# Both heads of a lone pair multiply whole float32 v into one PSUM tile, and ACT squares q and k: attention and two mixers on one core

## The chip, the core and the metric

The kernel runs on one core of a Trainium2 chip. It is one program; its time is the device time of one execution in microseconds (us). Before the change three runs took 1522.56, 1524.37 and 1529.31 us, so the median is 1524.37 us.

Engine names in the rows: PE is TensorE (matmul), PEld its weight load, DVE is VectorE, ACT is ScalarE, POOL is GpSimd, SP is SyncE, which issues nearly all DMAs here.

## The reference

Attention over q, k, v of shape (4 batches, 12 heads, 448 tokens, 64), with an RMS norm on q and k, then two mixer blocks:

```python
q_n, k_n = (rmsnorm(q, g_q), rmsnorm(k, g_k))
scores = scale * np.matmul(q_n, k_n.transpose(0, 1, 3, 2))
scores = scores - np.max(scores, axis=-1, keepdims=True)
attn = np.exp(scores)
attn = attn / (np.sum(attn, axis=-1, keepdims=True) + 1e-09)
x = np.matmul(attn, v)          # then heads are joined: (4, 448, 768)

h = x.transpose(0, 2, 1) @ U @ V                 # block a: rank 32 over tokens
u = x + h.transpose(0, 2, 1)
x = u + np.maximum(u @ w_ch1, 0.0) @ w_ch2       # 768 -> 3072 -> 768

h = np.maximum(x.transpose(0, 2, 1) @ w_tok1, 0.0) @ w_tok2   # block b
u = x + h.transpose(0, 2, 1)
x = u + np.maximum(u @ w_ch1b, 0.0) @ w_ch2b     # 768 -> 1536 -> 768
```

The weights arrive as 64-bit floats, read as pairs of 32-bit words.

## The kernel before

Heads are worked two by two: a pair is two neighbouring heads of one batch, its tiles hold both. There are 24 pairs. The first 12 (batches 0 and 1) run by themselves, one head after another; these are the lone pairs. The other 12 (batches 2 and 3) are interleaved by `run` with the channel mixer `ffn` of block a on batches 0 and 1. After that no attention is left. All steps are emitted in the order of the Python loops, and a scheduler then orders each engine's own queue; the order on each engine is fixed when the program is built, and an engine carries out its queue in that order.

A lone head goes through these steps:

- `fetch_heads` and `load_pair`: q, k and v of a pair are loaded by SP as 112 x (2 heads x 4 chunks x 64). POOL (DVE in turns 0, 2 and 3) squares q and k into `sq`, DVE sums the squares into `ms`, small operations make the inverse norm `rs`, and POOL multiplies q and k by it into `qn` and `kn`.
- `turn_pair`: PE transposes qn and kn into `tt`; ACT and DVE cut each into a rounded part and a rest (`both`), and SP copies them to `qs` and `ks`, so that one matmul of depth 128 takes both parts.
- `softmax`: for each of 4 chunks of 112 queries, two matmuls make the scores `sc`; DVE takes the negative maximum `nm` (L459), ACT the exponential `p` with its sum (L461), POOL scales `p` (L468).
- `weigh`: for each of 4 chunks of 112 keys, PE transposes the four `p` into `pt` (L487). Then p times v is summed in `pv`.

The product with v has two forms. The odd head of a lone pair, and both heads of a later pair, take the **split** form: ACT copies pt to `ph` as float32r (L498), DVE makes the rest `pl` (L502), v is split by ACT and POOL into `vs`, and two float32r matmuls, ph and pl, go to pv. The product lies in two halves of pv, so ACT copies one to `tmp` (L510) and DVE adds the other (L511). The even head of a lone pair takes the **whole** form: `ph` is a plain float32 copy of pt, made by ACT and DVE in turn (L498, L496), and one float32 matmul with `vr` follows. The profile records each such float32 matmul twice. DVE copies 64 rows of pv to the result (L507).

PSUM has 8 banks. In the lone stage 3 hold sc, 1 tt, and 4 are shared by pt and pv (`pools["v"] = pools["p"]`).

After the last lone pair comes what is called the seam below: `rank_mix` of batches 0 and 1 (the rank-32 mixer: lines L570 to L605, tiles `pt_x`, `xs`, `ps_h`, `ps_u`, `xT`, `u`), and the first two chunks of each channel weight of block a. Such a chunk is 768 KB in `w_raw`; `to_f32` converts it (ACT L130 and L135, DVE L131, L132 and L136, POOL L139), `split` cuts it into two float32r tiles (ACT L149, POOL L150), and these are stored as `h_a` for use again.

## Time and profile before

| | |
|---|---|
| median of three runs | 1524.37 us |
| lowest, highest | 1522.56, 1529.31 us |
| span of the profiled execution | 1530.0 us |
| PE busy | 1440.5 us (94%) |
| DVE busy | 1177.0 us (77%) |
| ACT busy | 745.0 us (49%) |
| POOL busy | 908.4 us (59%) |
| mean granted TensorE clock | 0.982 of full speed |

The span runs from the first to the last instruction of the profiled execution. For that execution no time of its own is given beside its span; the span is 5.6 us over the median of the three runs and 0.7 us over the highest. Busy shares are means over stages with different limits, so the table alone doesn't say what a stage waits for. Durations of matmuls overlap; what PE takes for one is read from the distance of starts.

### The profile page before, as it was taken

To read this page: it belongs to the slowest core of one execution; us is meant where nothing else is said; L and a number is where in the kernel's file an instruction comes from. 1 tells how busy PE (TensorE), PEld (TensorE's weight loads), DVE (VectorE), ACT (ScalarE), POOL (GpSimd) and SP (SyncE) were. 2 spreads that over 40 slices of the span, in tenths; PEclk is the share of its full clock that TensorE was granted. 3 is DMA by queue.
4 is the path that set the end of the run, shared out by engine and by line. 5 is a ranking of instruction groups with operands and counts; after the bars stand their busy time and mean duration, and the time that the engine had idled before them with its cause. 6 is when DMAs were issued, how large, how long until landed. Compare 5 with 4: busy or idle time off the path is not lost.

```text
span 1530.0 us, 22086 instructions
## 1 busy us (share of the span) xinstructions
PE 1440.5 (94%) x7396; PEld 1274.2 (83%) x7396; DVE 1177.0 (77%) x1805; ACT 745.0 (49%) x1508; POOL 908.4 (59%) x943
## 2 busy tenths in 40 slices
PE   4899988999899999999999999999999999999998
PEld 3666767888788889888888998898999998988997
DVE  7898888977787788676757776477888988577786
ACT  4687765765565665444535343335343431334431
POOL 5889947777666565455655454037787855206842
PEclk9999989999999999999999999999999999999999
DMA  6676656866666565765637664354545363423433
GB/s 174 156 168 158 151 169 208 273 201 199 223 207 202 165 207 189 248 228 189 213 125 239 227 232 143 115 194 130 181 125 185 125 192 122 130 92 109 137 117 108
DMA packets 144385, 266.06 MB, mean 174 GB/s; under 512 B 12832, under 2 KB 104448, under 8 KB 144160
## 3 DMA queue, kind: packets, MB, share of 16 engines
q1 hardware_dynamic: 143952, 264.65, 55.4%
q8 instruction: 59, 0.97, 0.3%
q14 instruction: 54, 0.44, 0.1%
q10 hardware_dynamic: 320, 0.00, 0.0%
HBM read 149.72 MB, written 79.10 MB: 150 GB/s over the span
## 4 chain that ended last, share of the span: by engine, by line
PE 50%; DVE 9%; DMA 4%; ACT 3%; POOL 3%; issue 2%; SPq 0%; DVEq 0%; POOLq 0%; ACTq 0%
PE ps_x L79 23%; PE ps_p L79 10%; PE ps_g L79 10%; PE ps_t L79 2%; PE ps_u L79 2%; DVE w_bits L136 1%; DVE w_bits L131 1%; DVE w_bits L132 1%; PE pv L79 1%; ACT w_bits L130 1%; POOL w L150 1%; DMA w_raw<-in_moe_w_ch_dram 1%; PE pt L487 1%; DMA c_a<-w_bits 1%; DMA qs<-both 1%
## 5 line engine op out<-in xcount | busy, mean ns | idle before, releaser
L79 PE MATMUL ps_x<-gs,w 128*128 128x448 f32 x1440 | 326.2, 373 | 7.6 <-DVE gs L656 2.9
L79 PE MATMUL ps_g<-u,w 128*128 128x448 f32 x1440 | 313.3, 371 | 6.5 <-DVE u L583 2.6
L79 PEld LDWEIGHTS ps_x<-gs,w 128*128 128x128 f32 x1440 | 268.6, 191 | 33.7 <-DVE gs L656 5.8
L79 PEld LDWEIGHTS ps_g<-u,w 128*128 128x128 f32 x1440 | 270.5, 190 | 30.3 <-DVE u L583 3.5
L79 PE MATMUL ps_x<-gs,w_b 128*128 128x448 f32 x1026 | 228.7, 368 | 6.5 <-DVE xT L851 2.0
L139 POOL TENSOR_TENSOR w_bits<-w_bits,w_round 128x768 uint32<-128x768 uint32 (+3 forms) x80 | 145.0, 1812 | 119.9 <-DVE w_bits L136 68.3
L79 PEld LDWEIGHTS ps_x<-gs,w_b 128*128 128x128 f32 x1026 | 192.7, 189 | 24.7 <-DVE xT L851 3.4
L150 POOL TENSOR_TENSOR w<-w_bits,w 128x768 fp32r<-128x768 f32 (+3 forms) x82 | 148.1, 1815 | 83.0 <-ACT w L149 78.6
L686 DVE TENSOR_TENSOR xT<-ps_x,xT 128x448 f32<-128x448 f32 x216 | 132.3, 618 | 44.5 <-PE ps_x L79 42.1
L150 POOL TENSOR_TENSOR w_b<-w_f,w_b 128x384 fp32r<-128x384 f32 x104 | 118.8, 1155 | 61.5 <-ACT w_b L149 61.1
L79 PE MATMUL sc<-ks,qs 128*112 128x448 f32 x384 | 124.6, 410 | 20.1 <-ACT p L461 16.9
L468 POOL TENSOR_SCALAR p<-p,sm 112x448 f32<-112x448 f32 x192 | 131.2, 696 | 19.4 <-DVE sm L465 16.1
L300 POOL TENSOR_TENSOR w_f<-w_f 128x384 f32<-128x384 f32 x26 | 36.4, 1401 | 178.7 <-DVE pu L779 73.5
L461 ACT ACTIVATE p<-sc,nm 112x448 f32<-112x448 f32 x192 | 121.4, 635 | 39.1 <-DVE nm L459 37.6
L459 DVE TENSOR_REDUCE nm<-sc 112x1 f32<-112x448 f32 x192 | 116.1, 614 | 11.8 <-PE sc L79 11.3
L487 PEld LDWEIGHTS pt<-ident,p 112*112 112x112 f32 x768 | 89.6, 135 | 34.3 <-issue 12.7
L487 PE MATMUL pt<-ident,p 112*112 112x112 f32 x768 | 110.6, 262 | 4.8 <-DVE pl L502 3.7
L498 ACT ACTIVATE ph<-pt 112x448 fp32r<-112x448 f32 (+1 forms) x168 | 88.2, 544 | 38.9 <-PE pt L487 38.0
L131 DVE TENSOR_SCALAR w_bits<-w_bits 128x768 f32<-128x768 f32 (+3 forms) x80 | 66.7, 834 | 50.0 <-ACT w_bits L130 50.0
L135 ACT ACTIVATE w_round<-w_raw 128x768 uint32<-128x768 uint32 (+3 forms) x80 | 69.8, 873 | 66.9 <-POOL w_bits L139 62.4
L502 DVE TENSOR_TENSOR pl<-pt,ph 112x448 fp32r<-112x448 f32 x144 | 86.9, 615 | 19.2 <-ACT ph L498 18.7
L130 ACT ACTIVATE w_bits<-w_raw 128x768 f32<-128x768 f32 (+3 forms) x80 | 70.0, 875 | 58.7 <-POOL w L150 31.4
(141 smaller groups left out, 2724.1 us busy)
## 6 DMA issues: line engine op xcount, KB each, us to landing
w_raw<-in_moe_w_ch_dram SPq DMA_DIRECT2D x72, 768.0 KB, 5.2
w_b<-h_a SPq DMA_DIRECT2D x65, 384.0 KB, 4.2
h_a<-w SPq DMA_DIRECT2D x56, 384.0 KB, 2.7
ks<-both SPq DMA_DIRECT2D x92, 224.0 KB, 3.7
c_a<-w_bits SPq DMA_DIRECT2D x40, 384.0 KB, 4.8
w_f<-c_a SPq DMA_DIRECT2D x40, 384.0 KB, 3.1
h_b<-w SPq DMA_DIRECT2D x32, 384.0 KB, 2.5
w_b<-h_b SPq DMA_DIRECT2D x29, 384.0 KB, 3.9
```

The costliest lines, as they stand in the source:

```text
L79: nc.tensor.matmul(o, lhsT=l, rhs=r, start=start, stop=stop)
L130: nc.scalar.activation(f(w), f(high), AF.Abs)
L131: nc.vector.tensor_scalar_max(f(w), f(w), TINY)
L139: nc.gpsimd.tensor_tensor(w, w, r, op=ALU.add)
L150: nc.gpsimd.tensor_sub(lo, w, f(hi))
L459: nc.vector.tensor_reduce(nm, sc, axis=AX.X, op=ALU.max, negate=True)
L461: nc.scalar.activation(p, sc, AF.Exp, bias=nm, accum_out=sm[:, c % 2:c % 2 + 1])
L468: nc.gpsimd.tensor_scalar(x, x, sm[:, i:i + 1], 1.0, op0=ALU.mult, op1=ALU.mult)
L487: nc.tensor.transpose(pt[:, c * CP:(c + 1) * CP], pr[c][:, kc * CP:(kc + 1) * CP], ident[:CP, :CP],)
L498: nc.scalar.activation(ph, pt, AF.Copy)
L502: nc.vector.tensor_sub(pl, pt, f(ph))
L686: nc.vector.tensor_add(xT[:, dc], px, xT[:, dc])
```

## The change

In the lone pairs both heads take the whole form. v is loaded into one of four standing tiles of shape 112 x 4 x 3 x 64 whose middle 64 columns are zero. The even head multiplies the first 128 columns (v, 0), the odd head the last 128 (0, v), and all eight matmuls of the pair add up in one `pv` of 128 rows, which DVE copies out once. v's load becomes two DMAs for each pair, with runs of 256 B in place of 1024 B. pv gets a PSUM bank of its own, and pt keeps three. ACT squares q and k in all lone pairs but those of turns 0, 2 and 3, with one buffer for q and another for k. The later pairs are as before.

```diff
-            t = pools["at"].tile([CP, 2, NC4, D], F32, tag="vr" if nm == "v" else "qkr", bufs=AT[nm + "r"],
-                        name=f"{nm}r")
-            nc.sync.dma_start(t, dict(q=q, k=k, v=v)[nm][b, h0:h0 + 2].rearrange(
-                "h (p c) d -> p h c d", c=NC4))
+            src = dict(q=q, k=k, v=v)[nm][b, h0:h0 + 2].rearrange("h (p c) d -> p h c d", c=NC4)
+            if nm == "v" and padded:
+                w = padded.pop(0)
+                padded.append(w)
+                for j in range(2):
+                    nc.sync.dma_start(w[:, :, 2 * j], src[:, j])
...
-            sq = pools["at"].tile([CP, 2 * NC4, D], F32, tag="sq", bufs=AT["sq"], name="sq")
+            sq = pools["pp" if padded and i else "at"].tile([CP, 2 * NC4, D], F32, tag="sq", bufs=AT["sq"], name="sq")
             tt = t.rearrange("p h c d -> p (h c) d")
-            mul(sq, tt, tt)
+            if padded and turn not in (0, 2, 3):
+                nc.scalar.activation(sq, tt, AF.Square)
+            else:
+                mul(sq, tt, tt)
...
     def split_v(vr, whole):
+        if whole:
+            return [vr[:, :, j:j + 2].rearrange("p c h d -> p c (h d)") for j in range(2)]
...
-        pv = psum("v", [P, S], "pv")
+        pv = joint.pop() if whole and j else psum("v", [P, S], "pv")
+        if whole and not j:
+            joint.append(pv)
...
-                mm(pv, vj[:, kc * D:kc * D + P], ph, kc == 0, kc == NC4 - 1)
+                mm(pv, vj[:, kc], ph, j == 0 and kc == 0, j == 1 and kc == NC4 - 1)
...
-            nc.vector.tensor_copy(dst[j * D:(j + 1) * D], pv[:D])
+            if j:
+                nc.vector.tensor_copy(dst, pv)
...
-        open_pools(inner, (("pp", 1, 0), ("s", 3, 1), ("t", 1, 1), ("p", 4, 1)))
-        pools["v"] = pools["p"]
+        open_pools(inner, (("pp", 1, 0), ("s", 3, 1), ("t", 1, 1), ("p", 3, 1), ("v", 1, 1)))
+        padded = []
+        for i in range(4):
+            padded.append(pools["pp"].tile([CP, NC4, 3, D], F32, tag=f"vp{i}", name="vr"))
+            nc.gpsimd.memset(padded[i][:, :, 1], 0.0)
```

The change also moves instructions on every engine, since the scheduler orders anew. Three places are shown. The lines of the changed kernel have other numbers: L487 becomes L498, L496 becomes L507, L507 becomes L519, L577 becomes L589, L581 becomes L593, L583 becomes L595.

On PE, in the middle of the lone stage, an odd head of before reads (pv_2012 is the odd head's, pv_2098 the next even head's; x4 and x2 are that many matmuls in a row):

```order
L79 MATMUL sc_2141<-ks_1964,qs_1963 112x448 x2
L79 MATMUL sc_2216<-ks_1970,qs_1969 112x448 x2
L79 MATMUL pv_2012<-pl_2061,vs_1545 128x448
L79 MATMUL pv_2012<-ph_2081,vs_1545 128x448
L487 MATMUL pt_2117<-ident_67,p_1881 112x112
L487 MATMUL pt_2117<-ident_67,p_1896 112x112
L487 MATMUL pt_2117<-ident_67,p_1916 112x112
L487 MATMUL pt_2117<-ident_67,p_1931 112x112
L79 MATMUL pv_2098<-ph_2104,vr_1552 128x448
L79 MATMUL pv_2012<-pl_2083,vs_1545 128x448
```

With the change, where one pair ends and the next begins (pv_1363 is the next pair's):

```order
L79 MATMUL sc_1371<-ks_1214,qs_1213 112x448 x2
L425 MATMUL tt_1622<-ident_67,qn_1476 128x112 x4
L498 MATMUL pt_1417<-ident_67,p_1132 112x112
L498 MATMUL pt_1417<-ident_67,p_1147 112x112
L498 MATMUL pt_1417<-ident_67,p_1167 112x112
L498 MATMUL pt_1417<-ident_67,p_1182 112x112
L498 MATMUL pt_1488<-ident_67,p_1290 112x112
L498 MATMUL pt_1488<-ident_67,p_1304 112x112
L79 MATMUL sc_1391<-ks_1214,qs_1213 112x448 x2
L79 MATMUL pv_1363<-ph_1369,vr_118 128x448
L79 MATMUL pv_1363<-ph_1388,vr_118 128x448
L79 MATMUL pv_1363<-ph_1404,vr_118 128x448
```

The matmuls with pl are gone, all products read vr, and the products of two pairs no longer interleave, since there is one bank for pv.

On SP, the first weight chunk of block a stands before the change behind every load and copy of the lone pairs (qs_2833 and ks_2834 belong to the second later pair):

```order
L442 DMA qs_2833<-both_2822 64x448 x2
L364 DMA vr_2713<-in_v_dram 112x2x256
L441 DMA ks_2834<-both_2830 64x896 x2
L364 DMA kr_3540<-in_k_dram 112x2x256
L364 DMA qr_3987<-in_q_dram 112x2x256
L364 DMA vr_2852<-in_v_dram 112x2x256
L121 DMA w_raw_2874<-in_moe_w_ch1_dram 128x6x128
L364 DMA vr_3542<-in_v_dram 112x2x256
L364 DMA vr_3991<-in_v_dram 112x2x256
L175 DMA h_a1_0_2888<-w_2884 128x768
```

With the change the second and third chunk (2674, 2953) are issued here, among the copies of the ninth lone pair (qs_1638 and qs_1644), and the first, w_raw_2657, stands 16 rows ahead of them:

```order
L367 DMA vr_118<-in_v_dram 112x4x64
L175 DMA h_a1_0_2671<-w_2667 128x768
L449 DMA qs_1638<-both_1627 64x448 x2
L367 DMA vr_118<-in_v_dram 112x4x64
L175 DMA h_a1_0_2671<-w_2668 128x768
L121 DMA w_raw_2674<-in_moe_w_ch1_dram 128x6x128
L121 DMA w_raw_2953<-in_moe_w_ch2_dram 128x768
L371 DMA qr_2135<-in_q_dram 112x2x256
L449 DMA qs_1644<-both_1627 64x448 x2
```

So the weight loads have moved ahead by several pairs, past copies that the lone pairs wait for; the fourth follows 7 rows below.

On DVE, at the start of the seam, the row before the change (L511 ends the last lone pair; L577 begins rank_mix):

```order
L511 TENSOR_TENSOR xT_82<-pv_2769,tmp_2814 64x448
L577 TENSOR_TENSOR xs_2940<-pt_x_2936,xs_2940 112x384
L577 TENSOR_TENSOR xs_2949<-pt_x_2945,xs_2949 112x384
L131 TENSOR_SCALAR w_bits_2876<-w_bits_2876 128x768
L132 TENSOR_SCALAR w_bits_2876<-w_bits_2876 128x768
L136 SCALAR_TENSOR_TENSOR w_bits_2876<-w_raw_2874,w_bits_2876 128x768
L577 TENSOR_TENSOR xs_2958<-pt_x_2954,xs_2958 112x384
L577 TENSOR_TENSOR xs_2967<-pt_x_2963,xs_2967 112x384
L605 TENSOR_TENSOR xs_2972<-ps_h_2935,xs_2972 64x384
```

With the change:

```order
L519 COPY xT_82<-pv_2534 128x448
L589 TENSOR_TENSOR xs_2724<-pt_x_2720,xs_2724 112x384
L589 TENSOR_TENSOR xs_2733<-pt_x_2729,xs_2733 112x384
L589 TENSOR_TENSOR xs_2742<-pt_x_2738,xs_2742 112x384
L589 TENSOR_TENSOR xs_2751<-pt_x_2747,xs_2751 112x384
L617 TENSOR_TENSOR xs_2756<-ps_h_2719,xs_2756 64x384
```

The conversion of the first weight chunk has left this place. So have those of the next three: all twelve DVE instructions of the four chunks now stand ahead of the last lone pair's copy, and so do their ACT operations L130 and L135, their POOL additions L139, and the split of the first two. The fifth chunk's three DVE instructions stand near the end of the last rank_mix.

## Rows read from the trace of the kernel before

**Rows 1.** Busy us of each engine by stretch: two lone, seam, mixed.

```profile
core 0: us, PE busy (x) PEld busy (x) DVE busy (x) ACT busy (x) POOL busy (x), PEclk, DMA share, GB/s
...
52.00:186.00 134.00, 122.68 (x704) 90.74 (x703) 116.23 (x241) 102.19 (x280) 120.26 (x225) 0.99 0.65 160
186.00:194.00 8.00, 6.30 (x34) 4.01 (x32) 5.35 (x9) 4.58 (x10) 6.05 (x11) 0.98 0.67 206
194.00:234.00 40.00, 33.42 (x152) 26.35 (x153) 34.82 (x58) 26.49 (x49) 17.47 (x12) 0.88 0.53 177
234.00:617.00 383.00, 363.54 (x1958) 323.18 (x1957) 307.39 (x522) 233.12 (x482) 255.17 (x283) 0.98 0.65 204
```

**Rows 2.** Groups of PE from 52 to 186 us: busy, mean ns, idle before.

```profile
L79 PE MATMUL sc<-ks,qs 128*112 128x448 f32 x146 | 47.5, 415 | 6.3 <-ACT p L461 4.7 <-DMA ks<-both 1.5
...
L79 PE MATMUL pv<-ph,vr 112*128 112x448 f32 x80 | 37.8, 554 | 0.0
...
L79 PE MATMUL pv<-pl,vs 112*128 112x448 f32 x40 | 17.6, 441 | 1.4 <-DVE pl L502 1.4
```

**Rows 3.** PE in order of time, 140 to 157 us: start, duration.

```profile
149.08 0.92 PE L79 MATMUL pv<-ph,vr 112*128 112x448 f32 x2
149.83 0.55 PE L487 MATMUL pt<-ident,p 112*112 112x112 f32 x4
150.15 0.64 PE L79 MATMUL sc<-ks,qs 128*112 128x448 f32 x2
150.63 0.92 PE L79 MATMUL pv<-ph,vr 112*128 112x448 f32 x2
...
155.23 0.45 PE L79 MATMUL pv<-ph,vs 112*128 112x448 f32 x1
155.52 0.37 PE L79 MATMUL pv<-pl,vs 112*128 112x448 f32 x1
155.73 0.55 PE L487 MATMUL pt<-ident,p 112*112 112x112 f32 x4
```

**Rows 4.** Groups of POOL, DVE and ACT from 52 to 186 us.

```profile
L468 POOL TENSOR_SCALAR p<-p,sm 112x448 f32<-112x448 f32 x80 | 51.0, 650 | 1.5 <-DVE sm L465 0.3 <-PE pt L487 0.2
...
L502 DVE TENSOR_TENSOR pl<-pt,ph 112x448 fp32r<-112x448 f32 x40 | 24.0, 613 | 2.2 <-ACT ph L498 2.1
...
L498 ACT ACTIVATE ph<-pt 112x448 fp32r<-112x448 f32 x40 | 20.9, 548 | 5.6 <-PE pt L487 5.5
...
L496 DVE COPY ph<-pt 112x448 f32<-112x448 f32 x20 | 12.3, 615 | 0.3
L378 POOL TENSOR_TENSOR sq<-qr 112x512 f32<-112x512 f32 x11 | 11.4, 1040 | 0.9
...
L150 POOL TENSOR_TENSOR vs<-vr,vs 112x256 fp32r<-112x256 f32 x10 | 7.3, 728 | 0.1
...
L511 DVE TENSOR_TENSOR xT<-pv,tmp 64x448 f32<-64x448 f32 x11 | 6.8, 618 | 1.9 <-ACT tmp L510 1.6
...
L510 ACT ACTIVATE tmp<-pv 64x448 f32<-64x448 f32 x10 | 5.4, 541 | 1.7 <-PE pv L79 1.4
```

**Rows 5.** SP's issues around the end of the lone stage.

```profile
189.59 0.45 SPq L121 DMA_DIRECT2D w_raw<-in_moe_w_ch_dram  x1
```

**Rows 6.** Groups of DVE, POOL and ACT in the seam, 194 to 234 us.

```profile
L583 DVE TENSOR_TENSOR u<-xT,u 128x448 fp32r<-128x448 f32 x10 | 8.9, 897 | 0.0
...
L139 POOL TENSOR_TENSOR w_bits<-w_bits,w_round 128x768 uint32<-128x768 uint32 x4 | 7.5, 1865 | 18.2 <-DVE w_bits L136 18.2
...
L130 ACT ACTIVATE w_bits<-w_raw 128x768 f32<-128x768 f32 x5 | 4.5, 906 | 0.9 <-DMA w_raw<-in_moe_w_ch_dram 0.9
...
L136 DVE SCALAR_TENSOR_TENSOR w_bits<-w_raw,w_bits 128x768 uint32<-128x768 uint32 x4 | 4.4, 1092 | 0.0
...
L131 DVE TENSOR_SCALAR w_bits<-w_bits 128x768 f32<-128x768 f32 x4 | 2.2, 560 | 0.7 <-ACT w_bits L130 0.6
L132 DVE TENSOR_SCALAR w_bits<-w_bits 128x768 uint32<-128x768 uint32 x4 | 2.2, 553 | 0.0
```

**Rows 7.** DMA from 20 to 195 us: the busiest queue; one issue group.

```profile
q1 hardware_dynamic: 19080, 28.16, 65.0%
...
vr<-in_v_dram SPq DMA_DIRECT2D x13, 224.0 KB, 2.9
```

**Rows 8.** Groups of ACT over the whole span: the table load.

```profile
L87 ACT ACT_TABLE_LOAD x1 | 1.3, 1283 | 0.7 <-PEq L1173 0.7
```

More of the change, by code (lines that the diff above doesn't have):

```diff
@@ L354, in w2_ring, with fetch_heads @@
         yield
-    def fetch_heads(b, hp, names):
+    def fetch_heads(b, hp, names, padded=None):
         h0 = 2 * hp
@@ L361, in fetch_heads, with load_pair @@
         for nm in names:
-            t = pools["at"].tile([CP, 2, NC4, D], F32, tag="vr" if nm == "v" else "qkr", bufs=AT[nm + "r"],
-                        name=f"{nm}r")
-            nc.sync.dma_start(t, dict(q=q, k=k, v=v)[nm][b, h0:h0 + 2].rearrange(
-                "h (p c) d -> p h c d", c=NC4))
-            res.append(t)
+            src = dict(q=q, k=k, v=v)[nm][b, h0:h0 + 2].rearrange("h (p c) d -> p h c d", c=NC4)
[5 more added lines that the diff above has]
+            else:
+                w = pools["at"].tile([CP, 2, NC4, D], F32, tag="vr" if nm == "v" else "qkr",
+                                     bufs=AT[nm + "r"], name=f"{nm}r")
+                nc.sync.dma_start(w, src)
+            res.append(w)
         return res
-    def load_pair(b, hp, turn, qk):
+    def load_pair(b, hp, turn, qk, padded):
         first = turn == 0
         mul = nc.vector.tensor_mul if turn in (0, 2, 3) else nc.gpsimd.tensor_mul
-        qr, kr, vr = qk + fetch_heads(b, hp, "v")
+        qr, kr, vr = qk + fetch_heads(b, hp, "v", padded)
         ms = pools["at"].tile([CP, 2, 8], F32, tag="ms", name="ms")
         for i, t in enumerate((qr, kr)):
-            sq = pools["at"].tile([CP, 2 * NC4, D], F32, tag="sq", bufs=AT["sq"], name="sq")
+            sq = pools["pp" if padded and i else "at"].tile([CP, 2 * NC4, D], F32, tag="sq", bufs=AT["sq"], name="sq")
             tt = t.rearrange("p h c d -> p (h c) d")
-            mul(sq, tt, tt)
+            if padded and turn not in (0, 2, 3):
+                nc.scalar.activation(sq, tt, AF.Square)
+            else:
+                mul(sq, tt, tt)
             nc.vector.reduce_sum(ms[:, i], sq, axis=AX.X)
@@ L403, in split_v @@
     def split_v(vr, whole):
+        if whole:
+            return [vr[:, :, j:j + 2].rearrange("p c h d -> p c (h d)") for j in range(2)]
         vs = pools["at"].tile([CP, 2, NC4, 2, D], F32R, tag="vs", bufs=AT["vs"], name="vs")
-        js = [j for j in range(2) if j not in whole]
-        if js:
-            js = slice(js[0], js[-1] + 1)
-            split(vr[:, js], vs[:, js, :, 0], vs[:, js, :, 1])
-        flat = vr.rearrange("p h c d -> p (h c d)")
-        return [flat[:, j * NC4 * D:] if j in whole else vs[:, j] for j in range(2)]
+        split(vr, vs[:, :, :, 0], vs[:, :, :, 1])
+        return [vs[:, j] for j in range(2)]
     def turn_pair(qn, kn, first=False, second=False):
@@ L511, in weigh, with attention @@
         nc.vector.tensor_add(dst[j * D:(j + 1) * D], pv[:D], tmp)
-    def attention(pairs, seam):
+    def attention(pairs, seam, padded):
         n = 2 * len(pairs)
@@ L536, in attention @@
                 steps.append(weigh(
-                    probs.pop(t), values[t // 2][t % 2], t % 2, dst, t % 2 in pairs[t // 2][2]))
+                    probs.pop(t), values[t // 2][t % 2], t % 2, dst, pairs[t // 2][2]))
             for _ in zip_longest(*steps):
@@ L558, in attention @@
                 loaded[h // 2] = load_pair(
-                    *pairs[h // 2][:2], h // 2, fetched.pop(h // 2))
+                    *pairs[h // 2][:2], h // 2, fetched.pop(h // 2), h < seam and padded)
                 if h == 0:
@@ L1069, in attention_then_two_mixers @@
         att = attention(
-            [(b, hp, (0,), lambda xT=xT, hp=hp: xT[:, hp], lambda dst: None)
+            [(b, hp, True, lambda xT=xT, hp=hp: xT[:, hp], lambda dst: None)
              for b, xT in zip((b0, b1), xs) for hp in range(NP)]
-            + [(b, hp, (), new_xo,
+            + [(b, hp, False, new_xo,
                 lambda dst, b=b, hp=hp: nc.sync.dma_start(xd[b][hp], dst))
-               for b in (b2, b3) for hp in range(NP)], 2 * H)
+               for b in (b2, b3) for hp in range(NP)], 2 * H, padded)
         for t in att:
```

1 line of the change is left out of this document (added).

## The prediction

> **What bounds the kernel now.** I read the busy times by stretch first. The change touches the lone pairs, so four stretches matter [rows 1]. Between 52 and 186 us there are 80 records of a whole product, two for each product and four products for each pair, so ten pairs pass in 134 us, 13.4 us each [rows 1, 2]. No engine is alone there: PE is busy 122.7 us of the 134, POOL 120.3, DVE 116.2, ACT 102.2. PE's own idle time, 134 - 122.7 = 11.3 us, is 1.1 us for each pair; the score matmuls carry 6.3 us of it, 4.7 of these in waiting for ACT's exponential [rows 2]. POOL is the fullest of the three helpers, with 12.0 us of work in a 13.4 us period. Then comes the seam, 194 to 234 us. There DVE is busy 34.8 of 40 us, POOL only 17.5, and the granted clock falls to 0.88 [rows 1]; DVE sets its pace. The rest of the span is the mixed stage, where PE is busy 363.5 of 383 us, and the later blocks, which the change leaves as they are.
>
> How long PE is taken up is read from the distance of starts in the order of time, since durations overlap [rows 3]. Four transposes take 149.83 to 150.15, 0.32 us. Two score matmuls take 0.48 us. One whole product takes 149.08 to 149.83, 0.75 us. A split product takes 0.29 for ph and 0.21 for pl (155.23 to 155.52 to 155.73), 0.50 us. For a pair of before: 8 groups of pt (2.6), 8 of sc (3.8), 4 whole (3.0) and 4 split products (2.0), and 2 groups of tt at the price of pt (0.6): 12.0 us of the 13.4.
>
> **The change part by part.** *PE.* Four split products become whole: 4 x (0.75 - 0.50) = +1.0 us a pair, 13.0 in all.
>
> *POOL* loses two squares of 1.04 and v's rest of 0.73: -2.8 us a pair [rows 4]. *DVE* loses four pl (0.613) and one of two output operations (0.618) and gains two copies of pt (0.615): -1.8. *ACT* loses two copies of pt (0.548) and tmp (0.541) and v's rounding, which is not in the rows and which I bound by nothing and by a copy of pt. It gains two squares of 112x512, an operation that before doesn't have on ACT: from a copy of 448 columns (0.548) upwards, with POOL's 1.04 as the far end; I take 0.62, by length 512/448 of the copy. ACT comes out between -0.4 and -0.9, or at about +0.4 by the far end.
>
> So in the lone stage the helpers get lighter, and PE becomes the fullest engine. What is its period? If PE never waited, 13.0. If all its present idle time stayed, 13.0 + 1.1 = 14.1. I take half of that idle time, because part of it is a chain through POOL and DVE that is now shorter, and part (the exponential) is a chain that stays: 13.6, that is +0.2 us on twelve pairs, **+2 us**. The bounds are 12 x (13.0 - 13.4) = -5 and, if the added work is wholly exposed, +12.
>
> *Moved weight loads.* Before, the first chunk of block a is issued at 189.59 us [rows 5], and its conversion, and that of three more, lies in the seam. The changed order has the four conversions inside the lone stage. That takes from DVE in the seam 2.2 + 2.2 + 4.4 = 8.8 us [rows 6]. It also takes POOL's 1.87 us operations away from beside it: the ten L583 in the seam take 0.897 us each, where an addition of the same length takes 0.618 [rows 4, 6]; I estimate that this 10 x 0.28 = 2.8 us goes too. DVE would have 34.8 - 8.8 - 2.8 = 23.2 us of work. I leave its present idle time of 5.2 in place, since that is the chain of rank_mix over PE and ACT, and add the fifth chunk (0.56 + 0.55 + 1.09 = 2.2), which now stands at its end: 30.6 us instead of 40, **-9.4 us**. If PE sets the seam, no more than its idle time there, 40 - 33.4 = 6.6, can go; if only the waits of both that fall together go, 3. The other end is 12, without the fifth chunk.
>
> What the moved work costs in the lone stage: four chunks are 8.8 us on DVE, about 4 x 2 x 0.91 = 7 on ACT and, with the two splits taken at the price of an addition, 6 x 1.87 = 11 on POOL [rows 6]. Spread over the pairs that is under 1.1 us a pair on any of them, less than POOL and DVE give up, so I cost it at nothing while PE is the fullest. Without that cover it would be 0.9 us a pair on POOL for twelve pairs. The transfers are another matter. SP's queue is in order, so each 768 KB chunk and each h_a store stands ahead of some qs and ks, and PE's scores wait for these. Now such waits are 1.5 us in ten pairs [rows 2]; four more of these would be up to 6 us at 1.5 each. That goes into the range, not into the sum.
>
> *The end of the lone stage* loses ACT's tmp (0.541) between the last product and the result: **-0.5 us**.
>
> *v's loads* are two for each pair, in runs of 256 B: 112 x 8 runs instead of 112 x 2, 672 more. The queue's 19080 packets took 65.0% of 16 engines over 175 us, 95 ns each on average [rows 7]. So the cost lies between nothing and 672 x 95 ns / 16 = 4 us of DMA time a pair. v is loaded several heads ahead of its use (`due(5)`) and lands in 2.9 us, so I take nothing. The Trainium skill ("DMA: Bandwidth & Descriptors", Specifications) speaks against these runs: it asks for at least 512 B in a transfer for full rate. No row here has a 256 B run; by that page the load would be slower, and the sum would stay the same as long as v is early. *The four memsets* stand at the start, while the first loads are under way (a load of this size lands after 2.9 us [rows 7]): nothing.
>
> **Sum.** -9.4 + 2 - 0.5 = -7.9 us. The profiled execution spans 1530.0 us, 5.6 over the median of the runs; the change of -7.9 against the median of 1524.4 gives **1516 us**.
>
> **The rivals.** *More gain.* POOL was the lid of the lone stage, and PE runs through at 13.0: -5, with the seam at -12: 1507. For it speaks POOL's 12.0 of 13.4; against it, that PE at no waiting has no row here.
>
> *No change.* The lone stage takes back what the seam gives: period 14.1 us, +8, by the idle time that stays or by qs and ks behind the weight chunks: 1524.4 - 9.9 + 8 = 1522. For it speaks that DMA is busy 0.65 of that stretch already [rows 1].
>
> *Slower.* One bank for pv. The first product of a pair must wait until DVE has copied the pair before it; PE's queue is in order, so the transposes and scores behind it wait too, and POOL and ACT for them. The price is the copy of 0.62 behind one other operation of DVE, 1.2 us a pair, on top of 1.0 wholly exposed: +2.2 x 12 = 26, less 9.9: 1541. It decides from a period of 14.9 us. Against it stands the changed order: two scores, four transposes of tt and six of pt are shown ahead of the next pair's first product, more than 1.2 us of work.
>
> *The squares make ACT change its tables.* The one table load takes 1.28 us [rows 8]. Two for each of nine pairs would be 23 us of ACT: up to 1539. The changed order has one load only, as before, so I give it little. The Trainium skill ("ScalarE: Activation LUTs", Table sets: the hidden batching unit) says that cheap functions are in every set, and names relu, copy, identity and abs; Square isn't among those named. By its 2.66 us for a switch the price would be 48 us; no row here shows a switch.
>
> **How the numbers follow.** Forecast (-3 to -14): 0.48. More gain: 0.17. No change: 0.21. Slower: 0.12. Tables: 0.02. About 0.5%, 7.6 us, is what a measurement of this kernel can tell from no change. Of the forecast's 0.48 some 0.30 lie beyond 7.6 us, and all of the greater gain: faster 0.47. Slower holds 0.14, the rest, 0.39, is no change. The range reaches from 1503, below the greater gain by some 4 us for what the new order does to the mixed stage, to 1530, the no-change case with all of the added product exposed; it leaves out most of the two slow cases. The forecast's own range is 1510 to 1521.
>
> **What would show it.** The lone stage: last copy to xT near 196 us (194 before), with PE busier than 92% and POOL down to some 10 us a pair. The seam: no L131, L132, L136 of the first four chunks in it, DVE's L595 at 0.62, and some 30 us from the last copy to the end of rank_mix. w_raw issued near two thirds of the lone stage. A wait of PE's pv for DVE's L519, or of sc for DMA ks, of over 10 us in all would make the prediction wrong; so would a mixed stage that is longer than 383 us by as much as the seam is shorter.

## The result and the profile after

The changed kernel is slower: 1541.72 us (median of 4 runs, 1539.27 to 1546.31) against 1526.84 us for the kernel before beside it (4 runs, 1522.56 to 1530.24). The ratio is 1.0109, with the interval [1.0071, 1.0147]. Forecast were 1516 us and a range up to 1530.

The profiled executions span 1530.0 and 1537.5 us, only 7.5 us apart where the medians are 14.9 apart. Other executions of the kernel before have spans from 1514 to 1529 us, so the profile of before is that of a long one. Stage times of single profiles are therefore read here only where they differ by more than some 5 us, or where several kernels repeat them; smaller differences are given, but little rests on them.

The first view gives busy times by stretch of the changed kernel, cut where [rows 1] cuts the kernel before: ten pairs from the first lone copy on, the eleventh to the twelfth, the seam, the mixed stage.

```profile
core 0: us, PE busy (x) PEld busy (x) DVE busy (x) ACT busy (x) POOL busy (x), PEclk, DMA share, GB/s
46.00:205.00 159.00, 145.43 (x738) 96.12 (x737) 115.59 (x235) 104.92 (x278) 121.23 (x221) 0.97 0.69 173
205.00:214.00 9.00, 8.97 (x43) 5.33 (x41) 3.88 (x8) 2.83 (x7) 3.59 (x9) 1.00 0.28 76
214.00:254.00 40.00, 31.38 (x151) 25.48 (x151) 30.95 (x52) 18.82 (x38) 7.58 (x6) 0.89 0.16 49
254.00:621.00 367.00, 353.45 (x1916) 314.58 (x1917) 295.23 (x509) 228.31 (x476) 254.77 (x279) 0.98 0.67 208
```

Ten pairs take 159 us where they took 134 [rows 1]; DVE and POOL have as much work in it as before, and more time. Groups of the lone stage, 46 to 214 us, which answer to [rows 2, 4, 6]:

```profile
L79 PE MATMUL pv<-ph,vr 112*128 112x448 f32 x176 | 83.0, 574 | 1.9 <-ACT ph L509 1.7
L79 PE MATMUL sc<-ks,qs 128*112 128x448 f32 x162 | 48.8, 401 | 7.1 <-ACT p L468 5.1 <-DMA ks<-both 1.9
...
L139 POOL TENSOR_TENSOR w_bits<-w_bits,w_round 128x768 uint32<-128x768 uint32 x4 | 8.2, 2046 | 0.5 <-ACT w_round L135 0.4
L433 DVE SCALAR_TENSOR_TENSOR both<-tt,gg,both 128x448 fp32r<-128x448 f32 x11 | 7.5, 681 | 15.9 <-ACT both L432 15.9
L432 ACT ACTIVATE both<-tt,gg 128x448 fp32r<-128x448 f32 x11 | 7.0, 633 | 18.8 <-DMA qs<-both 7.4 <-DMA ks<-both 4.2 <-PE pt L498 3.9
L385 ACT ACTIVATE sq<-kr 112x512 f32<-112x512 f32 x7 | 4.4, 632 | 1.9 <-DMA kr<-in_k_dram 1.8
...
L385 ACT ACTIVATE sq<-qr 112x512 f32<-112x512 f32 x6 | 3.8, 628 | 4.5 <-DMA qr<-in_q_dram 4.4
L130 ACT ACTIVATE w_bits<-w_raw 128x768 f32<-128x768 f32 x4 | 3.7, 918 | 7.1 <-DMA w_raw<-in_moe_w_ch_dram 4.9 <-POOL w L150 2.2
```

The square costs 0.63 us, as forecast. Neither of the two waits that the prediction named as its ruin is there: no product on PE waits for DVE's L519 (one weight load waits 0.5 us), and the scores wait 1.9 us for ks. What has grown is in the last rows: ACT stands still for q's and k's loads, for `both`, and for the weight chunks. Before the change its wait at `both` for SP's copies was small, from 51.7 us to the last lone copy:

```profile
L425 ACT ACTIVATE both<-tt,gg 128x448 fp32r<-128x448 f32 x10 | 6.4, 636 | 7.7 <-issue 4.2 <-DMA qs<-both 2.2 <-DMA ks<-both 1.0
```

The stages, from the starts of DVE's writes of a finished head or pair, in the order of time. The last lone copy (to xT, the result of the lone pairs) ends the lone stage; the first and last write to xo, the tile for a later pair's result, bound the mixed stage:

| us | first lone copy | last lone copy | first xo | last xo | end |
|---|---|---|---|---|---|
| before | 51.7 | 194.0 | 269.5 | 616.1 | 1530.0 |
| after | 45.9 | 213.8 | 278.9 | 620.6 | 1537.5 |

So the lone stage ends 19.8 us later; 10.4 us come back up to the first later pair, 4.9 in the mixed stage, and 3.0 are lost after it. The lone stage's length, 142.4 us before and 167.9 after, overstates its part: the first copy comes 5.8 us earlier, with more scores still to do behind it (162 records against 146). The expectations below speak of that length; the results are read mostly from its end. Where each head of a pair is copied out by itself, the first lone copy is that of the first pair's second head.

Six of the 768 KB transfers start inside the lone stage, from 102.6 to 156.7 us; the first four chunks are also converted there. One stretch shows a new kind of stop. SP, then ACT, then PE of the changed kernel, in order of time:

```profile
125.70 1.21 SPq L121 DMA_DIRECT2D w_raw<-in_moe_w_ch_dram  x2
```

```profile
133.93 0.90 ACT L130 ACTIVATE w_bits<-w_raw 128x768 f32<-128x768 f32 x1 [3.46 <-DMA w_raw<-in_moe_w_ch_dram]
134.74 0.90 ACT L135 ACTIVATE w_round<-w_raw 128x768 uint32<-128x768 uint32 x1
135.53 0.53 ACT L509 ACTIVATE ph<-pt 112x448 f32<-112x448 f32 x1
```

```profile
136.11 1.02 PE L79 MATMUL pv<-ph,vr 112*128 112x448 f32 x2 [1.66 <-ACT ph L509]
```

A chunk issued at 125.70 us has landed by 133.9; ACT's queue stands at it for 3.46 us, the copy to ph behind it starts late, and PE waits 1.66 us for that copy. The pair in which this lies, from 124.2 to 146.9 us, takes 22.7 us.

### The profile page after: what moved, and what is told of

Same layout as the page of the kernel before. It is cut to its first block, busy times and chain, and to the rows that moved or that the text cites. A ratio compares the mean times of both kernels' runs of the same rounds, so it can differ in the third digit from the quotient of the medians.

```text
span 1537.5 us, 21973 instructions
## 1 busy us (share of the span) xinstructions
PE 1455.5 (95%) x7396; PEld 1271.5 (83%) x7396; DVE 1156.1 (75%) x1769; ACT 731.2 (48%) x1478; POOL 885.3 (58%) x917
## 4 chain that ended last, share of the span: by engine, by line
PE 61%; DVE 12%; POOL 8%; DMA 7%; ACT 6%; issue 5%; SPq 1%; DVEq 0%; POOLq 0%; ACTq 0%
PE ps_x L79 24%; PE ps_g L79 12%; PE ps_p L79 10%; PE pv L79 4%; PE sc L79 3%; PE pt L498 2%; POOL w L150 2%; POOL w_bits L139 2%; DVE w_bits L131 2%; PE ps_u L79 2%; PE ps_t L79 2%; DMA qs<-both 2%; DVE w_bits L136 1%; DVE w_bits L132 1%; ACT w_bits L130 1%
## 5 line engine op out<-in xcount | busy, mean ns | idle before, releaser
L139 POOL TENSOR_TENSOR w_bits<-w_bits,w_round 128x768 uint32<-128x768 uint32 (+3 forms) x80 | 144.6, 1807 | 101.1 <-DVE w_bits L136 53.6
L475 POOL TENSOR_SCALAR p<-p,sm 112x448 f32<-112x448 f32 x192 | 137.7, 729 | 29.7 <-DVE sm L472 26.4
L79 PE MATMUL sc<-ks,qs 128*112 128x448 f32 x384 | 121.1, 407 | 21.2 <-ACT p L468 15.8
L498 PEld LDWEIGHTS pt<-ident,p 112*112 112x112 f32 x768 | 91.3, 136 | 51.7 <-issue 22.6
L498 PE MATMUL pt<-ident,p 112*112 112x112 f32 x768 | 114.0, 264 | 4.2 <-POOL p L475 2.7
L131 DVE TENSOR_SCALAR w_bits<-w_bits 128x768 f32<-128x768 f32 (+3 forms) x80 | 70.9, 886 | 57.7 <-ACT w_bits L130 57.5
L135 ACT ACTIVATE w_round<-w_raw 128x768 uint32<-128x768 uint32 (+3 forms) x80 | 70.0, 875 | 83.1 <-POOL w_bits L139 83.0
L79 PE MATMUL pv<-ph,vr 112*128 112x448 f32 x192 | 91.9, 581 | 5.5 <-ACT ph L509 5.3
L130 ACT ACTIVATE w_bits<-w_raw 128x768 f32<-128x768 f32 (+3 forms) x80 | 70.0, 875 | 57.0 <-POOL w L150 36.0
L79 PE MATMUL ps_p<-t,w_b 128*128 128x448 f32 x432 | 95.1, 366 | 0.1
```

The source lines that it names most:

```text
L79: nc.tensor.matmul(o, lhsT=l, rhs=r, start=start, stop=stop)
L130: nc.scalar.activation(f(w), f(high), AF.Abs)
L131: nc.vector.tensor_scalar_max(f(w), f(w), TINY)
L135: nc.scalar.activation(r, low, AF.Copy, scale=2.0 ** -29)
L139: nc.gpsimd.tensor_tensor(w, w, r, op=ALU.add)
L475: nc.gpsimd.tensor_scalar(x, x, sm[:, i:i + 1], 1.0, op0=ALU.mult, op1=ALU.mult)
```

## The experiments

The ratio is to runs of the kernel before on the same chip; "lone end" is the start of the last lone copy in the profiled execution (194.0 before, 213.8 after).

| kernel | median us | ratio to before, interval | lone end |
|---|---|---|---|
| a_hold | 1565.36 | 1.0281 [1.0243, 1.0319] | 207.9 |
| a_own_hold | 1558.55 | 1.0233 [1.0206, 1.0261] | 205.5 |
| b_act | 1544.71 | 1.0144 [1.0119, 1.0168] | 207.3 |
| b_one | 1533.24 | 1.0060 [1.0036, 1.0083] | 195.1 |
| a_poolsq | 1545.14 | 1.0117 [1.0090, 1.0145] | 209.4 |
| a_p8 | 1559.09 | 1.0206 [1.0177, 1.0235] | 224.4 |
| a_both2 | 1542.71 | 1.0100 [1.0070, 1.0130] | 212.6 |
| b_act_both2 | 1534.70 | 1.0058 [1.0034, 1.0082] | 193.8 |
| a_own_hold_poolsq | 1550.84 | 1.0185 [1.0156, 1.0214] | 199.5 |
| a_own_poolsq | 1535.79 | 1.0068 [1.0047, 1.0090] | 214.7 |
| a_best_p10 | 1540.59 | 1.0096 [1.0068, 1.0124] | 219.5 |
| b_both2 | 1533.39 | 1.0083 [1.0053, 1.0114] | 197.2 |
| b_early | 1537.63 | 1.0103 [1.0052, 1.0154] | 209.1 |
| a_hold13 | 1554.40 | 1.0206 [1.0167, 1.0245] | 219.3 |
| a_own_hold13_poolsq | 1541.84 | 1.0125 [1.0080, 1.0171] | 215.9 |
| b_split | 1552.50 | 1.0201 [1.0152, 1.0251] | 219.1 |
| a_tie | 1535.32 | 1.0096 [1.0058, 1.0134] | 216.5 |
| a_own_poolsq_tie | 1543.22 | 1.0141 [1.0100, 1.0183] | 215.3 |

The whole times carry something that the experiments don't mean to change: the order of the mixed stage differs from kernel to kernel, and it takes 336 us (b_early, a_own_poolsq) to 360 us (a_poolsq, a_hold13, b_both2) in the profiles, 347 before. So a whole time near another proves little, and the lone end is read beside it. Each lone end is that of one execution. For b_one and b_act_both2 it is the fastest one (1522.48 and 1527.50 us), 10.8 and 7.2 us below the median, so their lone ends may flatter them.

### Weight chunks held back, and one bank for pv

**a_hold**, the changed kernel with the chunks behind the last lone copy on SP:

```diff
-            ins = nc.sync.dma_start(o, d)
+            with tc.issue_after(pools["hold"].ins) if pools.get("hold") else nullcontext():
+                ins = nc.sync.dma_start(o, d)
...
-                    nc.sync.dma_start(f(ks[half]), f(kk[rows]))
+                    marks["ks"] = nc.sync.dma_start(f(ks[half]), f(kk[rows]))
...
+        pools["hold"] = marks["ks"]
         w1s = [w1_chunk("a", wa1, j) for j in range(G)]
```

> The changed kernel, with the block-a weight loads tied on SP behind the ks copies of the second later pair, where they stood before the change. Theory H (the weight chunks moved into the lone stage stretch it: qs and ks wait behind them): the lone stage, 168 us from the first pair's copy to the last in the changed kernel, falls back by 12 us or more, the seam grows by some 5, and the time comes to 1528 to 1534. Theory W (the whole product's added PE time is simply exposed, 1.0 to 1.4 us a pair): lone stage shorter by at most 6 us, the seam takes that back or more, time 1538 to 1547. Theory B (one bank for pv makes PE wait at each pair) says the same as W here.

**a_own_hold** is the same with a pv for each head out of the four shared banks:

```diff
-        pv = joint.pop() if whole and j else psum("v", [P, S], "pv")
+        pv = psum("v", [P, S], "pv")
...
-                mm(pv, vj[:, kc], ph, j == 0 and kc == 0, j == 1 and kc == NC4 - 1)
+                mm(pv, vj[:, kc], ph, kc == 0, kc == NC4 - 1)
...
-            if j:
-                nc.vector.tensor_copy(dst, pv)
+            nc.vector.tensor_copy(dst[j * D:(j + 1) * D], pv[j * D:(j + 1) * D])
```

> As a_hold, and pv is no longer joint: each head has its own pv from the four banks that pt and pv share, as before the change, and 64 rows are copied out for each head. Both heads stay whole, ACT squares stay. Theory B: faster than a_hold by 10 us or more, near 1528. Theory W: within 5 us of a_hold or slower, since PE's work is the same and DVE has 12 more copies of 0.6 us.

The first chunk was then issued at 245 and 243 us, not at 190 as before the change, and everything after the last xo took 952 and 951 us instead of 914: the hold was too long, and these whole times can't say what the moved chunks cost. The lone end came 5.9 us earlier, and another 2.4 without the joint bank.

### The squares alone, the bank alone

**b_act**, the kernel before with ACT's squares only:

```diff
-            mul(sq, tt, tt)
+            if seam_ and turn not in (0, 2, 3):
+                nc.scalar.activation(sq, tt, AF.Square)
+            else:
+                mul(sq, tt, tt)
```

> The kernel before with only the squares moved to ACT in the lone pairs but turns 0, 2 and 3, with two buffers. POOL loses 2.1 us a pair, ACT gains 1.24. If POOL was the lid of the lone stage before (the prediction's rival of more gain): faster by 5 us or more, 1515 to 1522. If PE's waits are chains through all engines (W): within 5 us of before, 1522 to 1532.

**b_one**, the kernel before with three banks for pt and one for pv:

```diff
-        open_pools(inner, (("pp", 1, 0), ("s", 3, 1), ("t", 1, 1), ("p", 4, 1)))
-        pools["v"] = pools["p"]
+        open_pools(inner, (("pp", 1, 0), ("s", 3, 1), ("t", 1, 1), ("p", 3, 1), ("v", 1, 1)))
```

> The kernel before with only the banks changed: three for pt, one of its own for pv, so that a head's first product waits until the head before it has been copied out (24 times, twice as often as in the changed kernel). Theory B: slower by 10 us or more, 1537 or above. Theory W or H: within 5 us of before.

The bank moves the lone end by 1.1 us in the profiled execution, where PE waits 2.6 us in all for DVE to read pv out; by the median the whole is 9.3 us slower, and where these go no profile shows. The squares alone move the lone end by 13.3, and the whole by about as much as the change does. The groups of ACT and PE in the lone stage of b_act show how:

```profile
L429 ACT ACTIVATE both<-tt,gg 128x448 fp32r<-128x448 f32 x10 | 6.3, 633 | 19.0 <-DMA qs<-both 14.4 <-issue 4.5
...
L79 PE MATMUL sc<-ks,qs 128*112 128x448 f32 x152 | 50.9, 423 | 17.7 <-ACT p L465 17.6
```

ACT comes to `both` while SP is still copying the pair before out of the same buffer. It waits 14.4 us for that, exponentials stand behind it, and PE's scores wait 17.6 us for exponentials (4.7 in [rows 2]).

### Is it the buffer? Squares back on POOL, a second buffer

**a_poolsq** undoes the squares in the changed kernel (the diff of b_act backwards, one buffer). **a_both2** adds a second pair of `both` buffers in the lone stage; to make room, p, the exponentials, has 8 buffers in place of 12. **a_p8** has the 8 buffers alone and is its control. **b_act_both2** adds the second pair to b_act (10 buffers of p):

```diff
-            both = pools["at"].tile([P, 2, S], F32R, tag="qq" if scale else "kk",
+            both = pools["pp" if pools.get("alt") and turned_n[0] % 2 else "at"].tile([P, 2, S], F32R, tag="qq" if scale else "kk",
...
-        AT.update(p=12, ph=4, pl=4)
+        AT.update(p=8, ph=4, pl=4)
```

> The changed kernel with the squares of q and k back on POOL (one buffer), everything else as in the change. Theory A (ACT's squares are what made the change slow, since they stand in ACT's in-order queue ahead of exponentials): 1522 to 1532 us, ratio below 1.005 to the kernel before, the lone stage from the first to the last pair's copy shorter than 155 us (167.9 with the change, 142.4 before). Rival W (the two more whole products of each pair and the single bank of pv set the pace, and the squares don't matter here): 1537 us or more, lone stage 163 us or more.

> The changed kernel with a second pair of buffers for the turned q and k (both) in the lone stage, so that ACT's copy into both need not wait until SP has copied the pair before it; to make room p has 8 buffers in place of 12. Theory A, in the form that ACT's queue stands still at this buffer with exponentials behind it: at least 6 us less than the run with 8 buffers of p alone. Rival L (ACT is delayed by the loads of q and k that the squares wait for, or by the sheer work of the squares): within 3 us of the run with 8 buffers of p alone.

> The changed kernel with 8 buffers of p in place of 12 and nothing else: the control for the run with two buffers of both. All theories: within 5 us of the changed kernel, 1537 to 1548 us; p's buffers were not seen to be waited for.

> The kernel before with ACT's squares alone and a second pair of buffers for the turned q and k (both), 10 buffers of p in place of 12. With the squares alone it was 1544.7 us. Theory A in the form of the buffer both: 1532 us or less, ACT's waits at both below 4 us (14.4 with the squares alone). Rival L: 1540 us or more, with ACT's waits moved to the squares (for the load of q or k).

In b_act the second buffer takes the lone end from 207.3 to 193.8 us, all that the squares had cost there (in the fastest execution), and the whole from 1544.7 to 1534.7, which is still 0.6% above the kernel before. In the changed kernel with 8 buffers of p it takes it from 224.4 to 212.6 us. That p's buffers don't matter, as all theories had it, was wrong: 8 in place of 12 cost 10.6 us at the lone end. The rows of b_act_both2 that answer to the two of b_act:

```profile
L432 ACT ACTIVATE both<-tt,gg 128x448 fp32r<-128x448 f32 x10 | 6.3, 635 | 5.5 <-DMA qs<-both 5.0 <-issue 0.5
...
L79 PE MATMUL sc<-ks,qs 128*112 128x448 f32 x152 | 48.7, 413 | 6.6 <-ACT p L468 5.6 <-ACT rs L388 0.8
```

But a_poolsq refutes the squares as the cause of the whole loss: without them the lone end is only 4.4 us earlier, and the whole, with a mixed stage of 359.8 us, no faster.

### The whole products alone, with and without the chunks

**a_own_hold_poolsq** joins the three edits above (own banks, squares on POOL, chunks held), **a_own_poolsq** leaves the hold out. **a_best_p10** is a_own_poolsq with second buffers of `both`, p=10 and three standing tiles of v, which are loaded anew too early, so that some pairs multiply another pair's v. **b_both2** is the kernel before with the second buffers alone.

> Of the change the whole products alone: the squares back on POOL with one buffer, a pv for each head out of the four shared banks with 64 rows copied out for each head, and the weight chunks of block a held back on SP behind the last lone copies. Its whole time says little, since the hold is longer than in the kernel before and costs some 36 us after the seam; the lone stage is what counts (142.4 us in the kernel before, 167.9 with the change). Theory S (the growth of the lone stage, 25.5 us, is a sum of four costs: products 11, single bank 5, squares 5, weight chunks 5): 151 to 156 us. Rival C (the whole products are as good as hidden, and squares, bank and weights cost more together than one by one): 147 us or less. Rival F (fewer helpers' work doesn't help, the products cost more than their time on PE): 158 us or more.

> The same without the hold: whole products, own pv of each head, squares on POOL, and the weight chunks inside the lone stage as with the change. Theory S: lone stage 156 to 161 us, first copy near 47, seam 60 to 66. Rival H (weights in the lone stage cost nothing once the squares and the single bank are gone): within 2 us of the lone stage of the held run. Whole time 1525 to 1545 us, by which order the mixed stage gets (341 to 360 us in the runs so far).

> The same as the run before it, with a second pair of buffers for the turned q and k, three standing tiles of v in place of four, and 10 buffers of p. Second buffers of both took 13 us from the lone stage with 8 buffers of p and 10 us with the squares in the kernel before. Theory B (both is a place where ACT's queue stands still, whatever ACT squares): lone stage 6 us or more shorter than in the run without them, down to 150 us or less; whole time possibly below the kernel before. Rival: within 3 us, if only the squares made both a wait.

> The kernel before with a second pair of buffers for the turned q and k in the lone stage and nothing else. Theory B: lone stage 136 to 140 us (142.4 before), whole time 1517 to 1524 us. Rival: lone stage 141 us or more, since before ACT's squares nothing waits for both; whole time within 6 us of before.

The products alone end the lone stage at 199.5 us, 5.5 later than before, about half of the 12 x 1.0 us more on PE. That isn't because the rest was absorbed: the first whole pair ends 5 us earlier (46.7 us, 51.7 before), and the eleven pairs behind it take 152.8 us against 142.3, 0.95 us more for each. With the chunks inside the lone stage the same kernel ends it at 214.7: the chunks cost 15.2. PE's groups up to the lone end, first held (from 46 us), then not (from 47.2 us):

```profile
L79 PE MATMUL pv<-ph,vr 112*128 112x448 f32 x176 | 82.1, 553 | 3.5 <-ACT ph L505 3.2 <-DVE ph L503 0.3
L79 PE MATMUL sc<-ks,qs 128*112 128x448 f32 x153 | 49.3, 414 | 3.3 <-ACT p L466 2.7 <-DMA ks<-both 0.5
```

```profile
L79 PE MATMUL pv<-ph,vr 112*128 112x448 f32 x176 | 85.3, 575 | 5.0 <-ACT ph L504 5.0
L79 PE MATMUL sc<-ks,qs 128*112 128x448 f32 x152 | 50.6, 427 | 9.1 <-ACT p L465 8.4 <-DMA ks<-both 0.6
```

The waits for ACT rise from 5.9 to 13.4 us. Theory S, a sum of four costs (products, bank, squares, chunks), fails: with the chunks in place the squares and the bank add nothing (214.7 without both, 213.8 with both); without the chunks they add 8.4 (199.5 and 207.9). Second buffers of `both` gain nothing where POOL squares (b_both2, a_best_p10).

### The chunks alone, and their old place

**b_early**, the kernel before with the chunks written earlier:

```diff
+            if t == 11:
+                pools["late"] = True
+                w1s = [w1_chunk("a", wa1, j) for j in range(G)]
+                pools["late"] = False
             if t == 2 * H - 1:
                 break
-        pools["late"] = True
-        w1s = [w1_chunk("a", wa1, j) for j in range(G)]
-        pools["late"] = False
```

> The kernel before with the weight chunks of block a written some six heads earlier in the program, so that SP issues the first four about where the changed kernel does (behind 69, 84, 85 and 88 copies of qs; 70, 86, 86 and on with the change, 111 to 115 before); nothing else of the change. Theory M (weight chunks inside the lone stage delay it by their transfers and by their conversions in the in-order queues): lone stage 150 to 158 us against 142.4, seam 64 to 69 against 75.5, so the whole within 6 us of before. Rival P (the step of the prediction: the chunks are as good as free in the lone stage): lone stage up to 146 us, seam the same 64 to 69, whole 1514 to 1520 us.

**a_hold13** and **a_own_hold13_poolsq** hold the chunks behind the 13th last copy of ks instead of the last.

> The changed kernel with the weight chunks of block a held back on SP behind an earlier copy than in the first such run, so that they come about where the kernel before has them (behind 106, 117 and 118 copies of qs). Theory M: lone stage near 163 us as with the long hold (167.9 with the change), seam 70 to 78, whole 1536 to 1548 us, about the changed kernel's: what the lone stage gains the seam loses. Rival: the long hold's loss was its own, and the hoist costs more than it gives: 1533 us or less.

> Of the change the whole products alone, as in the run with the long hold, with the weight chunks about where the kernel before has them. Theory: lone stage 151 to 156 us (152.8 with the long hold, 142.4 before, so +1.0 us a pair, all of it exposed), first copy near 47, seam 70 to 77; whole 1528 to 1545 us by the order that the mixed stage gets. Rival: the products cost more than their time on PE when nothing else is changed, lone stage 158 us or more.

In b_early the lone end is 209.1, 15.1 us later than before with nothing else changed, and the kernel is slower by as much as with the whole change (1.0103, 1.0109). Up to the first xo 3.2 us come back, not the 6.5 to 11.5 expected of the seam. Three stretches of b_early, and ACT and PE in the middle one:

```profile
135.00:140.00 5.00, 5.00 (x27) 3.50 (x26) 3.85 (x8) 4.09 (x12) 4.74 (x9) 1.00 0.92 231
140.00:145.00 5.00, 1.61 (x10) 1.02 (x9) 3.06 (x8) 2.06 (x5) 4.57 (x11) 1.00 0.95 323
145.00:150.00 5.00, 4.43 (x18) 3.79 (x19) 5.00 (x6) 4.24 (x11) 5.00 (x6) 0.50 0.43 118
```

```profile
143.40 0.90 ACT L130 ACTIVATE w_bits<-w_raw 128x768 f32<-128x768 f32 x1 [2.94 <-DMA w_raw<-in_moe_w_ch_dram]
144.19 0.90 ACT L135 ACTIVATE w_round<-w_raw 128x768 uint32<-128x768 uint32 x1
144.98 0.98 ACT L498 ACTIVATE ph<-pt 112x448 fp32r<-112x448 f32 x2
```

```profile
145.57 0.74 PE L79 MATMUL pv<-ph,vs 112*128 112x448 f32 x1 [3.96 <-ACT ph L498]
```

ACT stands at the chunk for 2.94 us, PE stands for 3.96 behind it, and the granted clock of the next 5 us is 0.50, the lower of its two levels (1.2 GHz). The two shorter holds missed their aim: the first four chunks came at 157 to 194 us, still ahead of a lone end at 216 and 219 us. They cost no less there than where the change has them: 16.4 us (215.9 against 199.5 with the long hold) beside 15.2 in the one kernel, 11.4 (219.3 against 207.9) beside 5.9 in the other.

### The wait or the work of the chunks

**a_tie** and **a_own_poolsq_tie** tie the first ACT operation of a chunk behind later exponentials:

```diff
-        nc.scalar.activation(f(w), f(high), AF.Abs)
+        tie = pools["tie"].pop(0) if pools.get("tie") else None
+        with tc.issue_after(marks["exp"][tie].ins) if tie else nullcontext():
+            nc.scalar.activation(f(w), f(high), AF.Abs)
```

> The changed kernel with the first ACT operation of each of the first four weight chunks (w_bits from w_raw) tied behind later exponentials of the lone pairs, so that the transfer of 768 KB has landed when ACT comes to it; the transfers are still issued inside the lone stage. In the changed kernel ACT waits 3.5 and 1.4 us for w_raw with copies and exponentials queued behind, and again 2.2 us for POOL's split. Theory Q (ACT's in-order queue stands still at w_raw, and PE behind it): ACT's waits for w_raw in the lone stage below 1 us and the lone stage 162 us or less (167.9 with the change). Rival R (the chunks cost by the work of their conversion and by their transfers beside qs and ks, not by this wait): lone stage 165 us or more although the wait is gone.

> The same ties in the kernel with whole products alone (own pv for each head, squares on POOL, weight chunks inside the lone stage; lone stage 167.4 us, 152.8 with the chunks held back). Theory Q: lone stage 161 us or less. Rival R: 164 us or more with ACT's waits for w_raw below 1 us.

Both are inconclusive. The wait went over to the second ACT operation on the same tile, which wasn't tied (a_tie, lone stage):

```profile
L137 ACT ACTIVATE w_round<-w_raw 128x768 uint32<-128x768 uint32 (+2 forms) x7 | 5.4, 778 | 3.7 <-DMA w_raw<-in_moe_w_ch_dram 3.7
```

The first operation waits for no chunk any more, the second 3.7 us (3.1 in the other kernel), and the lone end stays. In a_tie ACT also stands longer at `both`: 16.5 us for SP's copies to qs, 7.4 in the changed kernel.

### The opposite of the change

**b_split**, the kernel before with `(b, hp, ()` for `(b, hp, (0,)` in the list of lone pairs: the split form for both heads.

> The opposite of the change: the kernel before with the split product for both heads of every lone pair. PE gets 1.0 us less a pair, DVE four rests pl less two copies and ACT two more copies, POOL and ACT more of v's split. If PE's time in the lone stage is exposed one for one in both directions: lone stage 129 to 134 us (142.4 before) and a whole of 1513 to 1522 us. Rival: the helpers take its place, lone stage 140 us or more, whole 1524 us or more.

The rival holds. PE has less work for the products, but waits 15.4 us for ACT's ph in the lone stage, and the lone end is 219.1. ACT itself stands 17.2 us at `both` for SP's copies to qs (2.2 before), as in b_act.

## Why the prediction was wrong

**The step that failed** is "so I cost it at nothing while PE is the fullest": the four weight chunks inside the lone stage. At the lone end they cost 15.1 us in the kernel before alone (b_early) and 15.2 beside the whole products. Holding them back in the whole change gains only 5.9 (a_hold): there the squares and the bank cost 8.4 once the chunks are gone, so the share of each depends on the order in which the parts are taken out. The prediction looked for the chunks' cost in busy time (0.9 us a pair on POOL) and in the queue of SP (up to 6 us). In busy time the cover was there: POOL's work per unit of time didn't rise (121.23 of 159 us, 120.26 of 134 in [rows 1]), though POOL gave up less than was priced: ten of 21 squares stay in those ten pairs, since it squares for the later pairs meanwhile. But an engine with idle time still carries out its queue in order. A chunk of the changed kernel lands 7.8 us after its issue (median of six; 6.0 in b_early, 5.0 for those from 195 to 260 us before). ACT reaches two of the first four before they have landed and stands there for 4.9 us in all (3.2 in b_early, 6.2 in a_own_poolsq), with copies and exponentials that PE needs behind.

That wait is less than the 15 us. What PE shows from the first to the last lone copy, in the kernel before, in b_early and in the changed kernel:

```profile
51.70:194.00 142.30, 129.28 (x739) 95.04 (x737) 121.88 (x249) 107.07 (x289) 126.61 (x235) 0.99 0.65 162
```

```profile
50.00:209.10 159.10, 138.50 (x742) 100.25 (x739) 132.58 (x258) 114.81 (x297) 141.17 (x234) 0.94 0.70 180
```

```profile
45.90:213.80 167.90, 154.33 (x781) 101.55 (x779) 119.41 (x241) 107.84 (x285) 124.92 (x229) 0.97 0.67 168
```

In b_early PE idles 7.6 us more than before (20.6 against 13.0), and nearly the same matmuls keep it busy 9.2 us longer, at a mean granted clock of 0.94 against 0.99. Beside the whole products the split is alike: 7.2 us idle and 145.6 busy with the chunks held, 15.0 and 152.5 with them inside, 763 records both times, the clock 0.99 and 0.94. So about half of the chunks' cost is PE standing still, and half is PE taking longer for the same matmuls.

Two stops of PE in a_own_poolsq, 4.16 and 4.60 us, come right behind an L130 at which ACT stood (3.59 us, put down to POOL, and 4.80, to the chunk's load), and the granted clock is 0.50 from 120 to 125 us, after the first, and 0.60 and 0.72 in the two 5 us from 145 us, around the second and after it. How much of the rest is the conversions' work stays open: the ties didn't remove the wait.

In the changed kernel PE idles hardly more than before (13.6 us); its lone stage is longer by PE's busy time, 25 us with 42 more records. By the prediction's prices some 17 us of that are accounted for (an estimate: eleven pairs at 1.0, eight pairs of scores at 0.48, 21 transposes at 0.08); for the rest the rows show only a clock of 0.97 in place of 0.99.

**The seam** gave 10.4 us by the first xo; forecast 9.4 to the end of rank_mix. Its steps held where named: L595 takes 0.62 us but for the last one, and the first four chunks are gone from it. By the start of the last addition of rank_mix the gain is 5.0 (236.08 - 194.05 = 42.0; 250.89 - 213.84 = 37.1), about half of the 9.4 and near the bound that PE's idle time set:

```profile
194.05 0.62 DVE L511 TENSOR_TENSOR xT<-pv,tmp 64x448 f32<-64x448 f32 x1
...
236.08 0.92 DVE L583 TENSOR_TENSOR u<-xT,u 128x448 fp32r<-128x448 f32 x1
```

```profile
213.84 0.62 DVE L519 COPY xT<-pv 128x448 f32<-128x448 f32 x1 [1.65 <-PE pv L79]
...
250.89 3.40 DVE L595 TENSOR_TENSOR u<-xT,u 128x448 fp32r<-128x448 f32 x1
```

**The whole products** were a term of the right kind and too small: +0.2 us a pair was forecast, with half of PE's idle time kept, and 0.95 measured, near the bound of wholly exposed work. PE's idle time did fall to about half (13.0 to 7.2 us in eleven pairs), but its busy time rose by 16.3 us, with 24 more records, where 11 were priced. At the lone end this is +5.5, within the bounds given (-5, +12), because the first pair is done earlier.

**The squares**: their price was right, their place in ACT's queue was not looked at. Alone they cost 13 us at the lone end by the wait at `both`. In the changed kernel they cost 4.4 (a_poolsq), and without the chunks and the single bank 6.0 (a_own_hold, a_own_hold_poolsq); that the costs don't add up is measured, why isn't shown.

**The rivals.** "Slower" gave 1541 us, which the time met by luck, since its mechanism isn't what the rows show: the single bank costs 1.1 and 2.4 us at the lone end (b_one, a_own_hold), and PE's wait for the copy is nothing in the changed kernel, 1.1 to 1.2 us in a_tie and a_poolsq and 2.6 in b_one. The 9.3 us of b_one's median leave it open whether the bank costs time elsewhere. No table was changed: one load in the profile, as before. None of the versions beats the kernel before.

**Still open** are the whole time of the change with the chunks at their old place, since no hold put them there, and 7.4 of the 14.9 us between the medians, which the two profiles don't show.

## What to carry to other kernels

Free busy time on an engine isn't room for an operation that waits for a transfer: with an in-order queue, ask when its data lands, and what stands behind it. Moving work from a full engine to an idle one needs a look at the buffers that this engine waits for (a second buffer of `both` undid the cost of the squares at the end of their stage). When the order of a later stage changes with every build, read experiments by the stage they are about, and then check the whole.

## What was not expected of the hardware

The conversion on DVE costs more in the lone stage than in the seam: L131 took 1.24 us in b_early's lone stage, 0.56 in the seam before [rows 6].

```profile
L131 DVE TENSOR_SCALAR w_bits<-w_bits 128x768 f32<-128x768 f32 x4 | 4.9, 1237 | 1.7 <-ACT w_bits L130 1.7
```

POOL is busy 141 of 159 us there. The Trainium skill ("SBUF — State Buffer", SBUF: two separate sides) says that DVE, in some of its modes, and GpSimd lock a shared pair of ports for a whole instruction, and the other waits; the trace agrees in kind. So does the last L595 above, 3.40 us against 0.62: from 250.21 to 253.80 us POOL of the changed kernel carries out these two:

```profile
250.21 1.82 POOL L139 TENSOR_TENSOR w_bits<-w_bits,w_round 128x768 uint32<-128x768 uint32 x1
251.99 1.81 POOL L150 TENSOR_TENSOR w<-w_bits,w 128x768 fp32r<-128x768 f32 x1
```

v in runs of 256 B lands no sooner although each load is half as large: 3.4 us for 112 KB, where the 224 KB loads of q and k land after 3.7 and 3.6 us in the same stretch, and v's 224 KB before the change after 2.9 us [rows 7]:

```profile
vr<-in_v_dram SPq DMA_DIRECT2D x17, 112.0 KB, 3.4
```

This fits what the prediction cites of the Trainium skill ("DMA: Bandwidth & Descriptors", Specifications), but no run changes the length of the runs alone, and the loads of q and k take longer too (3.4 and 3.3 us before). It cost nothing that a row shows.
